# One transfer for a unit's rows, and a first weight matrix laid out as 128 long rows

## The chip, the cores and the metric

The kernel runs on one core of one Trainium2 chip. The metric is device time in microseconds (us) of one execution, taken as the median of several runs. Five engines work side by side on a core: TensorE (PE, with its weight loads shown apart as PEld), VectorE (DVE), ScalarE (ACT), GpSimd (POOL) and SyncE (SP), which here only issues transfers. The core has 16 DMA engines that move the bytes.

## The reference

Three layers follow each other. The first is a gated linear attention over 4 batches x 8 heads x 768 tokens of 40 values; its output is the 3,072 x 320 matrix that the second layer takes.

```python
for t in range(S):
    m_new = np.maximum(f_gate[:, :, t] + m, i_gate[:, :, t])
    f_stab = np.exp(f_gate[:, :, t] + m - m_new)
    i_stab = np.exp(i_gate[:, :, t] - m_new)
    C = f_stab * C + i_stab * outer(vt, kt);  n = f_stab * n + i_stab * kt
    y[:, :, t] = sigmoid(o_gate[:, :, t]) * (C @ qt) / np.maximum(np.abs(n @ qt), 1.0)
...
logits = x @ w_gate            # 8 experts, each takes its 384 best tokens, greedily
out[mask] = np.maximum(x[mask] @ w1[e], 0.0) @ w2[e]
...
h = x @ w_in                   # 320 x 2048, the "first weight matrix" (win)
g = np.where(h > 0.0, h, np.exp(np.minimum(h, 0.0)) - 1.0)
return g @ w_out               # 2048 x 320 (wout)
```

The weights `w_in` and `w_out` arrive as 8-byte floats and are turned into 4-byte ones on the chip.

## The kernel before

**Attention** runs over 24 units. A unit `u` is one chunk of 64 tokens (`n = u // 2`) of one pair of batches (`bp = u % 2`); the 128 partitions of its output tile `x` hold the 64 tokens of the one batch and the 64 of the other, the two in swapped order, since `values` and `recall` write to the opposite half (`64 - r`). `Attention.run` (L480 to L549) writes the order of all engines' work out by hand. In each unit it loads `vk` for unit u+4 and `qk` for unit u+5, both on SP's queue, multiplies, divides by the denominators in `gates` (L423, the last step is on POOL at L434), stores the unit's 128 rows of 320 values to the DRAM tile `xd` in `rows_out` (L436), and pulls one more piece of the late layers' weights (`pull`). The tile `x` has three buffers, `vk` six, `qk` four, a weight piece `cx` three.

**Weight pieces.** `win_pieces` (L987) brings in 15 pieces during attention: pieces 0 to 9 are `win`, pieces 10 to 14 the first part of `wout`. Each is loaded as 8-byte words (`fetch`, L942), turned into 4-byte floats (`conv`, L948) and split in two. Pieces 0 to 7 are 128 rows of 512 words. Pieces 8 and 9 are the last 64 rows of `win`, folded so that they fill 128 partitions: each has one transfer for the lower 64 partitions and one for the upper.

**SP's queue** runs in order. Each transfer on it uses one of eight semaphores in turn and waits until the transfer eight places ahead of it has landed.

**After attention** the router picks each expert's tokens (`Router.round`); the first round ends with gathers of rows from `xd` (`get_x`). Then the two expert layers run, eight rounds of 384 tokens each. The remaining nine pieces of `wout` (tile `wx`) are loaded from the end of attention on, behind the last store on SP's queue.

Of the kernel before, what the change touches and what calls it, by code (L numbers as in the profile page):

```python
# [16 lines left out]
B, H, S, D = 4, 8, 768, 40  # L17
# [102 lines left out]
class Attention:  # L120
# [315 lines left out]
    def rows_out(self, u):  # L436

        nc = self.nc
        n, bp = divmod(u, 2)
        x = self.st["x", u]  # L440
        for r in range(2):
            row = (bp * 2 + 1 - r) * S + n * 64
            nc.sync.dma_start(self.xd[row:row + 64], x[r * 64:r * 64 + 64])

    def turn(self, u):
        x = self.st.pop(("x", u))
# [105 lines left out]
class Router:  # L552
# [9 lines left out]
    def tables(self):  # L562
        nc, c, stage = self.nc, self.c, self.stage
        G, V = nc.gpsimd, nc.vector
        kw = dict(allow_small_or_imprecise_dtypes=True)
        self.pc = c.tile([128, 1], F32, name="pc")
        for r in (0, 64):
            G.iota(self.pc[r:r + 64], pattern=[[0, 1]], base=0, channel_multiplier=1, **kw)
        self.mul3 = c.tile([128, 3], F32, name="mul3")
        G.memset(self.mul3, -256.0)  # L570
        G.memset(self.mul3[:, 2:], -64.0)
        self.add3 = c.tile([128, 3], F32, name="add3")
        G.iota(self.add3[:, :2], pattern=[[128, 2]], base=2048, channel_multiplier=1, **kw)
        for h in (0, 64):
            G.iota(self.add3[h:h + 64, 2:], pattern=[[0, 1]], base=512, channel_multiplier=1, **kw)
        self.kx = c.tile([128, 32, 6], BF, name="kx")
        G.iota(self.kx, pattern=[[1, 32], [0, 6]], base=0, channel_multiplier=0, **kw)
        self.kl = c.tile([128, 16, 2], BF, name="kl")
        G.iota(self.kl, pattern=[[2, 16], [1, 2]], base=0, channel_multiplier=0, **kw)
        self.w8 = c.tile([128, 8], F32, name="w8")  # L580
        G.iota(self.w8, pattern=[[1, 8]], base=1, channel_multiplier=0, **kw)
        self.colv = c.tile([128, 24], BF, name="colv")
        for r in (0, 64):
            G.iota(self.colv[r:r + 64].rearrange("p (a b c) -> p a b c", a=2, b=2), pattern=[[64, 2], [2 * S, 2], [128, 6]],
                   base=(1 - r // 64) * S, channel_multiplier=0, **kw)
        jt = stage.tile([128, 128], I32, name="jt", bufs=1)
        G.iota(jt, pattern=[[1, 128]], base=0, channel_multiplier=0)
        d = stage.tile([128, 128], F32, name="tri0", bufs=1)
        G.iota(d, pattern=[[1, 128]], base=0, channel_multiplier=-1, **kw)
        self.ones = c.tile([128, 128], BF, name="ones")  # L590
        G.memset(self.ones, 1.0)
        self.onz = c.tile([128, 128], BF, name="onz")
        G.memset(self.onz, 64.0)
        G.memset(self.onz[0:1], 0.0)
        self.one48 = c.tile([128, 48], F32, name="one48")
        G.memset(self.one48, 1.0)
        self.ax = c.tile([128, 24], F32, name="ax")
        self.flag = [c.tile([128, 8], BF, name=f"flag{i}") for i in range(2)]
        for x in self.flag:
            G.memset(x, 0.0)  # L600
        yield
        self.thr0 = stage.tile([128, 128], I32, name="thr0", bufs=1)
        m = stage.tile([128, 128], I32, name="tblt", bufs=1)
        V.tensor_scalar(jt, jt, 25, None, op0=ALU.logical_shift_left)
        yield
        V.tensor_scalar(m, jt, 31, -1, op0=ALU.arith_shift_right, op1=ALU.bitwise_xor)
        yield
        V.tensor_scalar(m, m, -2**31, None, op0=ALU.bitwise_or)
        yield
        V.tensor_tensor(self.thr0, jt, m, op=ALU.bitwise_xor)  # L610
        yield
        V.memset(self.thr0[:, 0:1].bitcast(F32), -3.4e38)
        self.tri = c.tile([128, 128], BF, name="tri")
        V.tensor_scalar(self.tri, d, 0.0, -1.0, op0=ALU.is_gt, op1=ALU.add)
        yield
        self.far = c.tile([128, 128], BF, name="far")
        V.tensor_scalar(self.far, d, 0.0, -4096.0, op0=ALU.is_equal, op1=ALU.mult)
# [291 lines left out]
class Mlp:  # L909
# [77 lines left out]
    def win_pieces(self, stage):  # L987

        nc = self.nc
        A, G = nc.scalar, nc.gpsimd  # L990
        wide = self.win.dtype != F32
        n = 512
        al, lo, up = slice(0, 128), slice(0, 64), slice(64, 128)
        tiles = {}
        total = 10 + EARLY * 320 // 448
        self.piece = self.got = 0

        def whole():
            return stage.tile([128, n], F32, name="cF")

        def get(i):
            k, h = divmod(i, 4)
            cs = slice(h * n, h * n + n)
            tiles[i] = [stage.tile([128, n, 2], I32, name="cx", bufs=3) if wide else None, None, None if wide else whole()]
            if i >= 10:
                cs = slice((i - 10) * 448, (i - 10) * 448 + 448)
                tiles[i] = [t if t is None else t[:, :448] for t in tiles[i]]
                loads = [(al, self.src(self.wout, al, cs))]
            elif k < 2:
                loads = [(al, self.src(self.win, slice(k * 128, k * 128 + 128), cs))]  # L1010
            else:
                w = self.src(self.win, slice(256, 320), slice(h * 1024, h * 1024 + 1024))
                w = w.rearrange("p (k e t) -> e p k t", k=4, e=2)
                loads = [(lo, w[0]), (up, w[1])]
            self.fetch(loads, wide, tiles[i])

        def pull():
            if self.got < min(total, self.piece + 2 + wide):
                get(self.got)
                self.got += 1  # L1020

        self.pull = pull
        for i in range(total):
            self.piece = i
            while i not in tiles:
                yield
            k, h = divmod(i, 4)
            cs = slice((i - 10) * 448, (i - 10) * 448 + 448) if i >= 10 else slice(h * n, h * n + n)
            if wide:
                w = 448 if i >= 10 else n  # L1030
                tiles[i][1:] = stage.tile([128, n], F32, name="cg")[:, :w], whole()[:, :w]
            F = tiles[i][2]
            yield from self.conv(wide, tiles.pop(i), top=True)
            if i >= 10:
                A.activation(self.first[0][:, cs], F, AF.Copy)
                yield
                nc.vector.tensor_tensor(self.first[1][:, cs], F, self.first[0][:, cs], op=ALU.subtract)
            elif k < 2:
                A.activation(self.wih[:, k, cs], F, AF.Copy)
                yield  # L1040
                G.tensor_tensor(self.wil[:, k, cs], F, self.wih[:, k, cs], op=ALU.subtract)
            else:
                w = self.wis.rearrange("p (k e t) -> p k e t", e=2, t=128)[:, 4 * h:4 * h + 4]
                F = F.rearrange("p (k t) -> p k t", t=128)
                A.activation(w[lo, :, 0], F[lo], AF.Copy)
                yield
                A.activation(w[up, :, 1], F[up], AF.Copy)
                yield
                nc.vector.tensor_tensor(w[up, :, 0], F[lo], w[lo, :, 0], op=ALU.subtract)
                yield  # L1050
                nc.vector.tensor_tensor(w[lo, :, 1], F[up], w[up, :, 1], op=ALU.subtract)
            yield
# [500 lines left out]
def kernel(ctx, tc, qk, vk, ig, fg, wg, w1a, w1b, w2a, win, wout, out):  # L1553
# [22 lines left out]
    rt.__init__(nc, tc, consts, wk, L, sp, plan)  # L1576
    tables = rt.tables()
    next(tables)

    def hook(u):  # L1580
# [32 lines left out]
def _layout(i):  # L1613

    import numpy as np

    def by_dim(a):
        return a.reshape(2, 2, 8, 12, 64, 40).transpose(3, 1, 5, 0, 2, 4)

    def by_token(a):  # L1620
        return a.reshape(2, 2, 8, 12, 64, 40).transpose(3, 1, 4, 0, 2, 5)

    def words(a):
        a = np.ascontiguousarray(a)
        return a.view(np.uint64) if a.dtype == np.float64 else a

    d = {}
# [4 lines left out]
    v = by_token(i["v"])  # L1632
    v = np.concatenate([v, np.ones((*v.shape[:-1], 1), v.dtype)], -1)
# [6 lines left out]
    d["w1a"] = i["moe_w1"][:, :256].reshape(2048, 1024)  # L1640
    d["w1b"] = i["moe_w1"][:, 256:].reshape(512, 1024)
    d["w2a"] = i["moe_w2"].reshape(8, 2, 4, 128, 320).transpose(0, 1, 3, 2, 4).reshape(2048, 1280)
    d["win"] = words(i["moe2_w_in"])
    d["wout"] = words(i["moe2_w_out"].reshape(16, 128, 320).transpose(1, 0, 2).reshape(128, 5120))
    return {n: np.ascontiguousarray(a) for n, a in d.items()}

# [16 lines left out]
```

## Time and profile before

| | |
|---|---|
| median of 3 runs | 755.16 us (752.74 to 759.88) |
| profiled execution | 750.71 us |
| its span, first to last instruction | 748.9 us |
| PE busy | 702.9 us (94%) |
| DVE / ACT / POOL busy | 541.3 / 377.6 / 186.6 us |
| mean granted TensorE clock | 0.969 of full speed |

The table is read from the first part of the profile: the share of the span in which each engine is busy. PE is busy nearly throughout, but a mean over the span hides that the stages differ: attention takes the first 150 us, the router's first round some 35, the expert layers the rest.

### The profile page before, as it was taken

The numbers are of one execution on the slowest core, as the hardware profiler recorded it, in microseconds if no ns is written. First come the engines' busy times: TensorE is split into PE (matmuls) and PEld (weight loads), VectorE is DVE, ScalarE is ACT, GpSimd is POOL, SyncE is SP. The second block draws the span as 40 slices with busy tenths as digits, with TensorE's granted clock in tenths as the row PEclk, the third lists the DMA queues.
The fourth block names the chain that finished last, engine by engine and source line by source line (L and its number), as shares of the span: only waits on it lengthen the run. The fifth ranks groups of instructions, "written<-read, shape, count | busy, mean of one in ns | idle before, by whom it ended". The sixth has DMA issues, their size and how long they took to land.

```text
span 748.9 us, 17930 instructions
## 1 busy us (share of the span) xinstructions
PE 702.9 (94%) x7274; PEld 639.3 (85%) x7274; DVE 541.3 (72%) x1592; ACT 377.6 (50%) x804; POOL 186.6 (25%) x242
## 2 busy tenths in 40 slices
PE   7889888837999999999999999999999999999997
PEld 4656666626989999999999999999999999999997
DVE  8687888887898968965896698569868833851442
ACT  5455445435365725842772366256527743752443
POOL 5666655235111401210301120112022220001001
PEclk9899999957999999999999999999999999999999
DMA  7777968236002301400320230022013321100000
GB/s 280 237 231 226 251 212 261 51 109 214 18 1 85 124 1 51 131 28 1 103 80 28 85 93 5 27 85 98 1 30 109 112 88 45 36 1 26 1 2 27
DMA packets 22436, 67.31 MB, mean 90 GB/s; under 512 B 3536, under 2 KB 7632, under 8 KB 22352
## 3 DMA queue, kind: packets, MB, share of 16 engines
q1 hardware_dynamic: 14240, 35.12, 15.4%
q0 software_dynamic: 8064, 30.94, 12.4%
q8 instruction: 57, 0.93, 0.5%
q14 instruction: 27, 0.22, 0.1%
q10 hardware_dynamic: 48, 0.10, 0.0%
HBM read 58.28 MB, written 7.86 MB: 88 GB/s over the span
## 4 chain that ended last, share of the span: by engine, by line
PE 73%; issue 11%; DVE 9%; ACT 3%; POOL 2%; DMA 1%; POOLq 0%; SPq 0%; ACTq 0%; DVEq 0%
PE ph L1223 30%; PE acc L1362 6%; PE acc L1366 6%; PE acc L1363 6%; PE acc L1330 3%; PE acc L1332 3%; PE acc L1331 2%; PE pO L381 2%; PE pR L395 2%; PE pX L464 2%; PE acc L1317 1%; PE acc L1319 1%; PE pX L450 1%; PE pr L807 1%; PE pO L365 1%
## 5 line engine op out<-in xcount | busy, mean ns | idle before, releaser
L1276 DVE SCALAR_TENSOR_TENSOR e<-e,ph 128x384 f32<-128x384 f32 x128 | 70.3, 550 | 50.4 <-ACT e L1273 49.7
L1272 ACT ACTIVATE e<-ph 128x384 f32<-128x384 f32 x128 | 62.5, 488 | 79.4 <-PE ph L1223 74.3
L1223 PE MATMUL ph<-yh,wih 128*128 128x384 f32 x256 | 89.1, 348 | 0.7 <-DVE xl L1184 0.4
L1240 ACT ACTIVATE gh<-ph 128x384 fp32r<-128x384 f32 x64 | 31.3, 491 | 114.0 <-PE ph L1223 89.1
L1223 PE MATMUL ph<-yh,wil 128*128 128x384 f32 x256 | 86.1, 337 | 0.0
L1375 POOL DMA_INDIRECT out_dram<-ot,idx x24 | 24.0, 998 | 210.8 <-ACT ot L1093 207.8
L1100 DVE TENSOR_TENSOR gl<-e,gh 128x384 fp32r<-128x384 f32 x128 | 70.9, 561 | 1.8 <-ACT gh L1093 0.3
L1273 ACT ACTIVATE e<-e 128x384 f32<-128x384 f32 x128 | 67.3, 526 | 4.0
L1362 PE MATMUL acc<-woh,gh 128*128 128x320 f32 x216 | 68.3, 316 | 0.0
L1247 DVE SCALAR_TENSOR_TENSOR gl<-ph,gh 128x384 fp32r<-128x384 f32 x64 | 35.2, 552 | 45.5 <-ACT gh L1240 45.3
L1366 PE MATMUL acc<-woh,gl 128*128 128x320 f32 x216 | 66.9, 310 | 0.5 <-DVE gl L1100 0.5
L1363 PE MATMUL acc<-wol,gh 128*128 128x320 f32 x216 | 66.8, 309 | 0.0
L1223 PE MATMUL ph<-yl,wih 128*128 128x384 f32 x256 | 66.0, 338 | 0.0
L1093 ACT ACTIVATE gh<-e 128x384 fp32r<-128x384 f32 x96 | 49.0, 514 | 11.4 <-DVE e L1276 11.1
L1366 PE MATMUL acc<-woa,gl 128*128 128x320 f32 x168 | 52.4, 312 | 0.9 <-DVE gl L1100 0.9
L1362 PE MATMUL acc<-woa,gh 128*128 128x320 f32 x168 | 52.8, 314 | 0.0
L1223 PEld LDWEIGHTS ph<-yh,wih 128*128 128x128 f32 x256 | 48.1, 188 | 4.8 <-ACT yh L1335 4.1
L1363 PE MATMUL acc<-wob,gh 128*128 128x320 f32 x168 | 51.8, 308 | 0.0
L1223 PEld LDWEIGHTS ph<-yh,wil 128*128 128x128 f32 x256 | 48.1, 188 | 0.0
L1104 POOL DMA_INDIRECT stg<-in_w1a_dram,wi x16 | 15.7, 983 | 123.3 <-DVE wi L845 119.0
L1223 PEld LDWEIGHTS ph<-yl,wih 128*128 128x128 f32 x256 | 46.1, 188 | 0.0
L1223 PE MATMUL ph<-xh,w1h 128*128 128x384 f32 x128 | 44.6, 349 | 0.1
(290 smaller groups left out, 2041.4 us busy)
## 6 DMA issues: line engine op xcount, KB each, us to landing
vk<-in_vk_dram SPq DMA_DIRECT2D x24, 484.0 KB, 5.4
qk<-in_qk_dram SPq DMA_DIRECT2D x20, 320.0 KB, 5.5
cx<-in_win_dram SPq DMA_DIRECT2D x8, 512.0 KB, 5.1
xd<-x SPq DMA_DIRECT2D x48, 80.0 KB, 3.4
wx<-in_wout_dram SPq DMA_DIRECT2D x9, 320.0 KB, 3.0
cx<-in_wout_dram SPq DMA_DIRECT2D x5, 448.0 KB, 4.1
qk<-in_qk_dram SPq DMA_DIRECT2D x4, 512.0 KB, 6.1
cx<-in_win_dram SPq DMA_DIRECT2D x4, 256.0 KB, 5.7
```

The source lines that it names most:

```text
L1093: self.nc.scalar.activation(out, x, AF.Copy)
L1100: self.nc.vector.tensor_tensor(out, x, y, op=ALU.subtract)
L1223: PE.matmul(p, w, x, start=k == 0, stop=k == 7)
L1240: nc.scalar.activation(h, p, AF.Relu)
L1247: nc.vector.scalar_tensor_tensor(l, p, 0.0, h, op0=ALU.max, op1=ALU.subtract)
L1272: nc.scalar.activation(e, p, AF.Relu, scale=-1.0)
L1273: nc.scalar.activation(e, e, AF.Exp, scale=-1.0)
L1276: nc.vector.scalar_tensor_tensor(e, e, -1.0, p, op0=ALU.add, op1=ALU.max)
L1362: PE.matmul(p, h[:, c], wh, start=f == 0, stop=False)
L1363: PE.matmul(p, h[:, c], wl, start=False, stop=False)
L1366: PE.matmul(p, l[:, c], wh, start=False, stop=f == 15)
L1375: s = nc.gpsimd.indirect_dma_start(out=self.out, out_offset=bass.IndirectOffsetOnAxis(ap=idx[:, t:t + 1], axis=0), in_=o, in_offset=None)
```

## The change

`rows_out` stores a unit's rows in one transfer. For this the two batches of a pair change places in the inputs (q, k, v and the gates), so that after the swap inside the kernel partition half `r` belongs to batch `r`; on the DRAM side the 128 rows are then two blocks of 64 rows, 768 rows apart. The router's table of token numbers (`colv`) follows. `win` is laid out as 128 rows of 5,120 words: the first 128 rows of the matrix, the second 128, and the last 64 folded, side by side; so pieces 8 and 9 are loaded like the others, in one transfer of 128 rows each.

```diff
@@ -438,9 +438,8 @@  rows_out
         n, bp = divmod(u, 2)
         x = self.st["x", u]
-        for r in range(2):
-            row = (bp * 2 + 1 - r) * S + n * 64
-            nc.sync.dma_start(self.xd[row:row + 64], x[r * 64:r * 64 + 64])
+        rows = self.xd[bp * 2 * S:bp * 2 * S + 2 * S].rearrange("(r s) d -> r s d", r=2)
+        nc.sync.dma_start(rows[:, n * 64:n * 64 + 64], x)
@@ -582,7 +581,7 @@  Router.tables
             G.iota(self.colv[r:r + 64].rearrange("p (a b c) -> p a b c", a=2, b=2), pattern=[[64, 2], [2 * S, 2], [128, 6]],
-                   base=(1 - r // 64) * S, channel_multiplier=0, **kw)
+                   base=r // 64 * S, channel_multiplier=0, **kw)
@@ -999,19 +998,14 @@  win_pieces, get
-            k, h = divmod(i, 4)
-            cs = slice(h * n, h * n + n)
+            cs = slice(i * n, i * n + n)
             tiles[i] = [stage.tile([128, n, 2], I32, name="cx", bufs=3) if wide else None, None, None if wide else whole()]
             if i >= 10:
                 cs = slice((i - 10) * 448, (i - 10) * 448 + 448)
                 tiles[i] = [t if t is None else t[:, :448] for t in tiles[i]]
                 loads = [(al, self.src(self.wout, al, cs))]
-            elif k < 2:
-                loads = [(al, self.src(self.win, slice(k * 128, k * 128 + 128), cs))]
             else:
-                w = self.src(self.win, slice(256, 320), slice(h * 1024, h * 1024 + 1024))
-                w = w.rearrange("p (k e t) -> e p k t", k=4, e=2)
-                loads = [(lo, w[0]), (up, w[1])]
+                loads = [(al, self.src(self.win, al, cs))]
             self.fetch(loads, wide, tiles[i])
@@ -1614,6 +1608,10 @@  _layout
+    i = dict(i)
+    for n in ("q", "k", "v", "i_gate", "f_gate", "o_gate"):
+        i[n] = i[n].reshape(2, 2, *i[n].shape[1:])[:, ::-1].reshape(i[n].shape)
@@ -1640,7 +1638,8 @@
-    d["win"] = words(i["moe2_w_in"])
+    w = i["moe2_w_in"]
+    d["win"] = words(np.concatenate([w[:128], w[128:256], w[256:].reshape(64, 8, 2, 128).transpose(2, 0, 1, 3).reshape(128, 1024)], 1))
```

On PE, DVE, ACT and POOL the same instructions stand in the same order as before. Only SP's queue differs: it has 99 rows in place of 125. The two fences below show it at two places, by the order of the built program; a row names the tile written, the one read, the shape of the DRAM side, outermost count first, and in brackets what the transfer waits for (`DMAHW0` to `DMAHW7` are the eight semaphores of the queue's transfers, `Pool`, `DVE` and `Activation` those of the engines).

SP's queue in the middle of attention before, from the store of unit 9 to that of unit 10:

```order
L443 DMA xd<-x 64x320 [waits DMAHW2_49,Pool_49]
L443 DMA xd<-x 64x320 [waits DMAHW3_49]
L946 DMA cx<-in_win_dram 64x4x256 [waits DMAHW4_49,Activation_49]
L946 DMA cx<-in_win_dram 64x4x256 [waits DMAHW5_49]
L282 DMA vk<-in_vk_dram 128x968 [waits DMAHW6_49,DVE_49]
L278 DMA qk_114<-in_qk_dram 80x1024 [waits DMAHW7_49,DVE_49]
L443 DMA xd<-x 64x320 [waits DMAHW0_49,Pool_49]
L443 DMA xd<-x 64x320 [waits DMAHW1_49]
```

The same place with the change:

```order
L442 DMA xd<-x 2x64x320 [waits DMAHW1_49,Pool_49]
L945 DMA cx<-in_win_dram 128x1024 [waits DMAHW2_49,Activation_49]
L282 DMA vk<-in_vk_dram 128x968 [waits DMAHW3_49,DVE_49]
L278 DMA qk_114<-in_qk_dram 80x1024 [waits DMAHW4_49,DVE_49]
L442 DMA xd<-x 2x64x320 [waits DMAHW5_49,Pool_49]
```

Two stores of 64 rows have become one whose outermost count is 2, and the two loads of piece 8 one of 128 rows. Since a unit now has four transfers, the eighth transfer ahead is the same kind of transfer two units earlier.

SP's queue at the end of attention with the change, from the last load for attention (`vk` of unit 23) to the first loads of the rest of `wout`:

```order
L282 DMA vk<-in_vk_dram 128x968 [waits DMAHW4_49,DVE_49]
L442 DMA xd<-x 2x64x320 [waits DMAHW5_49,Pool_49]
L442 DMA xd<-x 2x64x320 [waits DMAHW6_49,Pool_49]
L442 DMA xd<-x 2x64x320 [waits DMAHW7_49,Pool_49]
L442 DMA xd<-x 2x64x320 [waits DMAHW0_49,Pool_49]
L442 DMA xd<-x 2x64x320 [waits DMAHW1_49,Pool_49]
L945 DMA wx<-in_wout_dram 128x640 [waits DMAHW2_49,Activation_49]
L945 DMA wx<-in_wout_dram 128x640 [waits DMAHW3_49,DVE_49]
L945 DMA wx<-in_wout_dram 128x640 [waits DMAHW4_49]
```

The five stores of units 19 to 23 stand there where ten transfers of 64 rows stood, and the `wx` loads still follow right behind.

## Rows read from the trace of the kernel before

**Rows 1.** The page's 40 equal slices of the span, in tenths.

```profile
PE   7889888837999999999999999999999999999997
DMA  7777968236002301400320230022013321100000
```

**Rows 2.** Busy time by stage (us); the last three columns are granted clock, DMA share, GB/s.

```profile
0.00:20.00 20.00, 14.83 (x281) 8.89 (x285) 16.78 (x39) 10.56 (x24) 10.81 (x43) 1.00 0.80 280
20.00:150.00 130.00, 113.03 (x3189) 84.22 (x3189) 103.78 (x247) 65.19 (x134) 69.55 (x71) 0.93 0.71 209
150.00:185.00 35.00, 18.73 (x163) 14.58 (x164) 26.46 (x93) 13.63 (x31) 16.72 (x17) 0.62 0.51 161
185.00:749.00 564.00, 556.36 (x3650) 531.66 (x3648) 394.25 (x1215) 288.17 (x616) 89.48 (x112) 1.00 0.16 51
136.50:148.00 11.50, 9.85 (x204) 8.24 (x202) 10.16 (x30) 4.22 (x12) 2.19 (x3) 1.00 0.20 46
```

**Rows 3.** The page's chain that ended last, by engine and by line.

```profile
PE 73%; issue 11%; DVE 9%; ACT 3%; POOL 2%; DMA 1%; POOLq 0%; SPq 0%; ACTq 0%; DVEq 0%
PE ph L1223 30%; PE acc L1362 6%; PE acc L1366 6%; PE acc L1363 6%; PE acc L1330 3%; PE acc L1332 3%; PE acc L1331 2%; PE pO L381 2%; PE pR L395 2%; PE pX L464 2%; PE acc L1317 1%; PE acc L1319 1%; PE pX L450 1%; PE pr L807 1%; PE pO L365 1%
```

**Rows 4.** Timeline of SP's queue: start, us, what was issued.

```profile
19.17 1.15 SPq L443 DMA_DIRECT2D xd<-x  x2
...
31.13 1.09 SPq L443 DMA_DIRECT2D xd<-x  x2
...
39.28 1.09 SPq L443 DMA_DIRECT2D xd<-x  x2
...
128.16 0.33 SPq L282 DMA_DIRECT2D vk<-in_vk_dram  x1
130.76 17.99 SPq L443 DMA_DIRECT2D xd<-x  x10
148.84 1.49 SPq L946 DMA_DIRECT2D wx<-in_wout_dram  x3
```

**Rows 5.** DMA view: SP's queue q1, and its transfers (count, KB each, us to landing).

```profile
q1 hardware_dynamic: 14240, 35.12, 15.4%
...
vk<-in_vk_dram SPq DMA_DIRECT2D x24, 484.0 KB, 5.4
qk<-in_qk_dram SPq DMA_DIRECT2D x20, 320.0 KB, 5.5
cx<-in_win_dram SPq DMA_DIRECT2D x8, 512.0 KB, 5.1
xd<-x SPq DMA_DIRECT2D x48, 80.0 KB, 3.4
...
cx<-in_wout_dram SPq DMA_DIRECT2D x5, 448.0 KB, 4.1
...
cx<-in_win_dram SPq DMA_DIRECT2D x4, 256.0 KB, 5.7
```

**Rows 6.** The tile xd: its stores and its gathers (min/median/max ns, first and last start).

```profile
L443 SPq DMA_DIRECT2D xd<-x x48: 445/508/1762, 19.2 to 148.2; - x48
L1104 POOL DMA_INDIRECT xg<-xd,idx x24: 942/950/1405, 174.1 to 598.4; - x24
...
DMA to landing us min/median/max: 2.0/3.1/6.2
```

**Rows 7.** Timeline of ACT: the last unit's gates from its vk tile, first use of wx.

```profile
141.50 0.47 ACT L355 ACTIVATE sg<-vk 128x320 f32<-128x320 f32 x1
...
152.15 0.48 ACT L958 ACTIVATE wt<-wx 128x320 f32<-128x320 f32 x1 [1.58 <-DMA wx<-in_wout_dram]
```

**Rows 8.** Busy time in two neighbouring stretches of attention, columns as in Rows 2.

```profile
24.00:31.00 7.00, 4.13 (x108) 2.93 (x111) 5.40 (x12) 5.99 (x12) 3.76 (x3) 0.93 0.80 245
31.00:39.00 8.00, 8.00 (x212) 6.12 (x212) 3.57 (x10) 2.31 (x5) 3.65 (x5) 0.63 0.64 178
```

**Rows 9.** The list of waits: POOL's step in gates behind stores.

```profile
POOL x L434 <- DMA xd<-x: 7.3, 3, 2.9
```

## The prediction

> **What bounds the kernel now.** I read the 40 slices first [rows 1]. PE is near nine tenths everywhere but in a hole around slices 9 and 10; the DMA line is high in slices 1 to 7 and low after them. So the transfers matter in attention, if anywhere. The table by stage says how much [rows 2]: from 185 us on PE is busy 556.36 of 564 us, and the chain that ended last is mostly the experts' matmuls [rows 3]. Nothing that the change touches works in that stage, so it moves as a block. From 20 to 150 us PE is busy 113.03 of 130 us, DVE 103.78, and the 16 DMA engines 0.71 of the time. Attention is thus close to three limits at once. Its pace is read from SP's queue [rows 4]: the store of unit 0 is issued at 19.17 us, that of unit 19 at 130.76, which is 111.59 / 19 = 5.87 us a unit. What delays the end of attention delays everything behind it.
>
> **Part by part: pieces 8 and 9.** Four loads of 256 KB become two of 512 KB. Same bytes; a 512 KB piece lands in 5.1 us, a 256 KB half in 5.7 [rows 5]. Rows of 40 KB pitch, as `win` now has, are what `wout` has already, and its 448 KB pieces land in 4.1 us, so the pitch costs nothing. The pieces are read long after they land. I count 0; two SP issues of some 0.5 us are saved on a queue that mostly waits for POOL and DVE.
>
> **The inputs' swap and the iota's base** change values, not instructions: 0.
>
> **The store.** Before, a unit has two stores of 80 KB, 64 rows each; all 48 are issued in 445 to 1762 ns and land 2.0 us after issue at best, 3.1 in the median [rows 6]. Now one of 160 KB. What decides is over how many of the 16 engines it is dealt out. Every transfer on SP's queue before has an outermost count that 16 divides (128, 80, 64, 32 rows), and none shows an engine left out. The new store is the first whose DRAM side has an outermost count of 2: two blocks of 64 rows. If a transfer is dealt out by whole outermost entries, two engines carry 64 rows each and 14 carry none.
>
> The Trainium skill says this outright (DMA: Bandwidth & Descriptors, section "Why a DMA increments its semaphore by 16 and not by 1"): the number of engines is the largest one up to 16 that divides the slowest dimension of both sides. By it the store runs on two engines. No run here shows such a transfer yet.
>
> I take two engines as likeliest, and price it. Bytes per engine and unit: `vk` 484/16 = 30.3 KB, `qk` 320/16 = 20.0, pieces (10 x 512 + 5 x 448)/16 over some 20 units = 23.0; together 73.3 KB. The stores add 10 KB to each of 16 engines before, and 80 KB to each of two after.
>
> What an engine moves while busy has three rows. In the first 20 us, loads alone, 280 GB/s at share 0.80 is 280/(16 x 0.80) = 21.9 GB/s, or 21.4 KB/us [rows 2]. Over all of q1, 35.12 MB in 15.4% of 16 x 748.9 us is 19.0 GB/s, 18.6 KB/us [rows 5]. From 136.5 to 148 us, where nearly all traffic is stores, 46/(16 x 0.20) = 14.4 GB/s, 14.0 KB/us [rows 2]. As a check, 83.3 KB at 18.6 is 4.5 us of a 5.87 us unit, 0.76; the table has 0.71.
>
> On the two engines a unit then takes:
> - low: everything at 21.4, 73.3/21.4 + 80/21.4 = 3.4 + 3.7 = 7.2 us;
> - middle: loads at 21.4, since the other 14 engines are idle half the time, and stores at 18.6, 64 packets in a row being nearer to the mean of the queue than to its short bursts: 3.4 + 4.3 = 7.7 us;
> - high: loads at 18.6, stores at 14.0, 3.9 + 5.7 = 9.6 us.
>
> Each load spreads over all 16 engines, so it lands only when the two slow ones have done their part; the unit's pace becomes theirs. Over the present 5.87 us that is +1.3, +1.86, +3.8 us a unit, and over 19 units with loads +25, +35, +72 us.
>
> Against this stands the lead of the loads. The last `vk` is issued at 128.16 us and lands 5.4 us later [rows 4, 5]; ACT reads it at 141.50 [rows 7]. So 141.5 - 133.6 = 7.9 us can pass before anything waits. Left: +17, +27, +64 us. SP's own waits put no further brake on: a transfer waits for the one eight ahead, which is now two units back, and two units of transfers in flight keep both engines fed.
>
> **The end of attention.** Units 20 to 23 have no loads; they take 17 us from 130.76 to the store's last issue at 148.2 [rows 4, 6]. Four stores on two engines take 4 x 3.7 to 4 x 5.7 = 15 to 23 us, in the middle 17: no change there. But the first `wx` load is issued right behind the last store and ACT waited 1.58 us for it already [rows 7], so no slack is left: the last store's 4.3 us in place of 80 KB over 16 engines (10/18.6 = 0.5) delays it by some 3 us (0 to 6). That wait passes to the router's round through ACT and DVE. The gathers of `xd` begin at 174.1 us, 26 us after the last store's issue [rows 6], more than its landing takes.
>
> **The clock.** After a stretch with PE busy 4.13 of 7.00 us the granted clock was 0.63 over the next 8 us, part of them at 1.2 GHz in place of 2.4, and the unit there took 39.28 - 31.13 = 8.15 us with PE busy throughout [rows 4, 8]. At 7.7 us a unit PE would be busy 5.1 of them (113.03/130 x 5.87), 66%, near that 59%. So some units will run at 8.15 in place of 7.7: at most 19 x 0.4 = 8 us, I take 4; nothing at the high end, where 9.6 us covers it.
>
> **Sum.** Low 17 + 0 + 0 = +17; middle 27 + 3 + 4 = +34; high 64 + 6 + 0 = +70 us. Against the profiled execution, 750.7 + 34 = 785 us; the median of the runs lies 4.4 us above that execution, so 755.2 + 34 = 789 us for a median.
>
> **Rivals.**
>
> *All 16 engines carry the store* (the 128 partitions of `x` decide, not the two blocks). Then 10 KB per engine and unit as before, and one SP issue of some 0.5 us less each unit. For it speaks that both forms move the same 128 rows of 1,280 bytes. It gives 755 us, not slower. The most it could win: POOL's step in `gates` is put down as waiting 7.3 us for stores, in three places [rows 9]; if all of it were theirs and went, 748 us, 1.0% faster. But POOL's operand comes from DVE's step just ahead of it (L433), and a wait for several is put down to the one that came last, so I believe little of it.
>
> The Trainium skill's "Rules for kernel authors" on the same page advise this side: small transfers are to be joined, and two halves of the partitions to be made one transfer. Taken alone that would give the 755 us here or a little less.
>
> *Two engines, but hidden.* The lead covers 7.9 us in 19 units, 0.4 us a unit. So a unit could take 6.3 us on the two engines and nothing would be seen: with loads at 3.4 that leaves 2.9 us for 80 KB, 28 KB/us, faster than any row's 21.4. It decides below that rate, and gives 755 to 760 us.
>
> *Deeper trouble.* Landing times on the two engines grow to two units, 15 us, about the distance between a piece's load and its first use; if ACT, in order, then stands at a piece's conversion, the unit waits for more than its bytes. That is past the high end: 825 us and up.
>
> **How the numbers follow.** Two engines and visible: 0.72, since the built program carries the count of 2 and every row before agrees with a deal by whole outermost entries without proving it. All 16 engines: 0.20. Two engines but hidden: 0.05. Deeper trouble: 0.03. The likeliest case alone spans 755 + 17 to 755 + 70, 772 to 825; packets could move a little faster than the slow rows say when 14 engines stand idle, so its own weight lies in the lower half. To hold 8 in 10 the range must reach into the case of 16 engines: from 754, which leaves out about half of that case, 0.10, to 816, which leaves out 0.08. About 1% is what a measurement of this kernel can tell from no change, its runs lying 752.74 to 759.88 us apart. Faster by over 1% is only the top of the first rival, 0.03; within 1% the rest of it and the hidden case, 0.22; slower 0.75.
>
> **What would show it.** Right: the `xd` stores land in 7 us or more in place of 3.1; `vk`, `qk` and pieces land in 10 us or more; the mean DMA share from 20 to 150 us falls well under 0.71; SP's queue waits for transfers; units are 7 to 8 us apart; the experts' stage keeps its 556 us of PE. Wrong: stores landing in about 3 us, and units still 5.9 us apart. If the stores land late but units keep their pace, the lead was larger than I read; if units pass 9.6 us, a wait behind an in-order engine adds to the bytes.

## The result, and the profile after

| | before | with the change |
|---|---|---|
| median | 756.82 us (4 runs) | 762.28 us (4 runs, 760.43 to 767.01) |
| ratio | | 1.0106, 95% interval 1.0063 to 1.0149 |
| profiled execution | 750.71 us | 760.43 us |
| its span | 748.9 us | 758.6 us |

The change makes the kernel slower by about 1%, 8 us by the ratio. The forecast was 789 us, 34 more than before, with a range of 754 to 816: the sign and the mechanism hold, the size does not. The unaltered kernel, run again in the experiments (run 7), gave 1.0095. The profiled execution of before, 750.71 us, lies under all four of its runs here, so the two spans differ by more, 9.7 us, than the medians do.

The page's slices of the changed kernel answer to [rows 1]:

```profile
PE   7898888754999999999999999999999999999997
DMA  7776666225300500500230121022003321100000
```

The high part of the DMA line is as long as before, but one to three tenths lower in three of its seven slices, and the hole in PE begins a slice earlier and is wider: 7, 5, 4 in slices 8 to 10, before 8, 3, 7. The table by stage answers to [rows 2] and [rows 8]; its last three columns are the granted clock, the DMA share and GB/s:

```profile
0.00:20.00 20.00, 15.44 (x276) 9.65 (x276) 16.36 (x38) 10.34 (x24) 10.11 (x42) 0.91 0.79 269
20.00:150.00 130.00, 110.62 (x3120) 81.36 (x3118) 99.24 (x223) 63.50 (x129) 66.82 (x70) 0.92 0.63 207
185.00:749.00 564.00, 560.27 (x3655) 533.65 (x3655) 400.00 (x1224) 291.91 (x624) 92.73 (x113) 1.00 0.16 54
...
142.00:150.00 8.00, 5.62 (x91) 4.43 (x85) 5.05 (x12) 3.83 (x10) 1.03 (x1) 0.79 0.13 45
...
149.00:156.70 7.70, 6.09 (x86) 5.22 (x86) 5.46 (x20) 1.92 (x6) 1.46 (x2) 0.88 0.13 42
```

From 144 to 157 us, when the last load has landed, only stores are left. In the last two rows the 16 engines have a mean share of 0.13, which is 2 of 16, and move 45 and 42 GB/s. I read this as two engines at some 22 GB/s each and 14 idle ones. Before, the same stores moved 46 GB/s at a share of 0.20 [rows 2], so the share alone does not count engines; the packets do, in runs 3 and 4. The queue's packets and its store row answer to [rows 5]:

```profile
q1 hardware_dynamic: 12720, 35.12, 14.1%
...
xd<-x SPq DMA_DIRECT2D x24, 160.0 KB
```

Of the 14,240 packets 1,520 are gone for the same 35.12 MB: 768 because pieces 8 and 9 come in packets of 4 KB in place of 1 KB, the other 752 smaller than 512 bytes. Times to landing are read here from the chain, the waits and the times at which the trace has each transfer's completions. SP's queue, to be held against [rows 4]:

```profile
19.89 0.63 SPq L442 DMA_DIRECT2D xd<-x  x1
...
49.76 0.50 SPq L442 DMA_DIRECT2D xd<-x  x1
...
129.93 0.49 SPq L442 DMA_DIRECT2D xd<-x  x1
130.51 2.83 SPq L945 DMA_DIRECT2D cx<-in_wout_dram  x1
133.43 2.14 SPq L282 DMA_DIRECT2D vk<-in_vk_dram  x1
135.67 20.98 SPq L442 DMA_DIRECT2D xd<-x  x5
156.74 1.36 SPq L945 DMA_DIRECT2D wx<-in_wout_dram  x3
```

The five stores from 135.67 on are those of units 19 to 23. From the store of unit 0 to that of unit 19 it is 115.78 us, before 111.59: +4.2. From there to the first `wx` load it is 21.07 us, before 18.08: +3.0. The store of unit 0 itself is 0.7 later. The first gather of `xd` comes at 183.8 us in place of 174.1 [rows 6], another +1.8 behind the `wx` load:

```profile
L442 SPq DMA_DIRECT2D xd<-x x24: 482/497/1737, 19.9 to 156.2; - x24
L1098 POOL DMA_INDIRECT xg<-xd,idx x24: 948/954/1414, 183.8 to 608.1; - x24
```

From that gather to the last instruction both kernels take 574.8 us. So the 9.7 us between the two spans are 0.7 + 4.2 + 3.0 + 1.8, all of them ahead of the experts' layers. These are single executions. Before and the kernels below with no store on two engines (runs 2, 3, 4, 6 and 11) took 111.0 to 119.0 us from the store of unit 0 to that of unit 19, so the 4.2 is not clear of their spread. From there to the first `wx` load they took 16.3 to 18.3 us, so the 3.0 is clear of it; from that load to the gather they took 25.3 to 26.8 against 27.1 here, so the 1.8 hardly is.

The list of waits, from the store of unit 0 to the router (us in total, times, longest):

```profile
ACT cg L957 <- DMA cx<-in_wout_dram: 8.2, 2, 5.0
PEld pS L306 <- DMA qk<-in_qk_dram: 7.7, 7, 1.8
...
ACT wt L957 <- DMA wx<-in_wout_dram: 2.8, 1, 2.8
```

Engines now wait for loads, ACT for weight pieces and PE for `qk`. The chain that ended last shows the longest of these waits, in unit 20 (start, us, what):

```profile
130.51 12.59 DMA cx<-in_wout_dram
143.12 0.05 ACT cg L957
```

The last weight piece is issued at 130.51 us, behind the store of unit 18 on the two engines, and lands 12.6 us later; before, such a piece took 4.1 us in the median [rows 5]. Of its 16 completions 14 are there by 136.44 us, the other two come at 140.43 and 143.10: two engines hold it back. ACT, in order, has nothing else to do:

```profile
143.12 0.60 ACT L957 ACTIVATE cg<-cx 128x448 f32<-128x448 f32 x1 [5.03 <-DMA cx<-in_wout_dram]
```

### The profile page after: what moved, and what is told of

Same layout as the page of the kernel before. It is cut to its first block, busy times and chain, and to the rows that moved or that the text cites. A ratio compares the mean times of both kernels' runs of the same rounds, so it can differ in the third digit from the quotient of the medians.

```text
span 758.6 us, 17883 instructions
## 1 busy us (share of the span) xinstructions
PE 709.1 (93%) x7274; PEld 644.2 (85%) x7274; DVE 542.7 (72%) x1592; ACT 377.8 (50%) x804; POOL 184.8 (24%) x242
## 2 busy tenths in 40 slices
DMA packets 20915, 67.30 MB, mean 89 GB/s; under 512 B 2784, under 2 KB 5856, under 8 KB 20832
## 3 DMA queue, kind: packets, MB, share of 16 engines
q1 hardware_dynamic: 12720, 35.12, 14.1%
## 4 chain that ended last, share of the span: by engine, by line
PE 70%; DVE 10%; issue 10%; DMA 6%; ACT 2%; POOL 1%; POOLq 0%; SPq 0%; ACTq 0%; DVEq 0%
PE ph L1217 30%; PE acc L1356 6%; PE acc L1360 6%; PE acc L1357 6%; PE acc L1324 3%; DMA qk<-in_qk_dram 3%; PE acc L1326 2%; PE acc L1325 2%; PE pR L395 2%; PE pO L381 2%; DMA cx<-in_wout_dram 2%; PE pX L463 2%; PE acc L1311 1%; PE acc L1313 1%; PE pS L306 1%
## 5 line engine op out<-in xcount | busy, mean ns | idle before, releaser
L1087 ACT ACTIVATE gh<-e 128x384 fp32r<-128x384 f32 x96 | 49.0, 514 | 11.5 <-DVE e L1270 11.1
L1098 POOL DMA_INDIRECT stg<-in_w1a_dram,wi x16 | 15.8, 986 | 123.3 <-DVE wi L844 119.0
```

The lines of the kernel that those rows point to most:

```text
L1087: self.nc.scalar.activation(out, x, AF.Copy)
```

## The experiments

All ratios are to the kernel before, run on the same chip beside them. Lines that begin with "-" are those of the changed kernel.

**1. The changed store alone.** `win`'s layout and its loads are those of before.

```diff
-                loads = [(al, self.src(self.win, al, cs))]
+            elif k < 2: loads = [(al, self.src(self.win, slice(k * 128, k * 128 + 128), cs))]
+            else: ... loads = [(lo, w[0]), (up, w[1])]
-    d["win"] = words(np.concatenate([w[:128], w[128:256], ...], 1))
+    d["win"] = words(i["moe2_w_in"])
```

> The changed store alone, with the first weight matrix laid out and loaded as before. Theory (the store runs on two of the 16 engines, and their time decides): all of the loss is here, the ratio to before is 1.006 to 1.015 as with the whole change, and during the last units the DMA share is 0.13, two of 16. Rival (the new layout of the weight matrix or its 512 KB pieces cost the time): the time is that of before, ratio 0.995 to 1.005.

Measured: 768.72 us, ratio 1.0184 (1.0157 to 1.0211). The loss is all in the store, and it is larger without the new layout than with it, which neither theory said.

**2. The new layout alone.** The rows go out in two transfers as before.

```diff
-        rows = self.xd[bp * 2 * S:bp * 2 * S + 2 * S].rearrange("(r s) d -> r s d", r=2)
-        nc.sync.dma_start(rows[:, n * 64:n * 64 + 64], x)
+        for r in range(2):
+            row = (bp * 2 + r) * S + n * 64
+            nc.sync.dma_start(self.xd[row:row + 64], x[r * 64:r * 64 + 64])
```

> The new layout of the first weight matrix alone; a unit's rows go out in two transfers of 64 rows as before. Theory (two engines): ratio to before 0.995 to 1.005, units of 5.9 us, and no stretch in which the DMA share stands at 0.13. Rival (layout): ratio 1.006 to 1.015.

Measured: 752.95 us, ratio 0.9978 (0.9949 to 1.0006): no difference that can be told.

**3 and 4. The same single transfer over four and over 16 engines.** Only the number of blocks on the DRAM side changes.

```diff
-        rows = self.xd[bp * 2 * S:bp * 2 * S + 2 * S].rearrange("(r s) d -> r s d", r=2)
-        nc.sync.dma_start(rows[:, n * 64:n * 64 + 64], x)
+        rows = self.xd.rearrange("(r s) d -> r s d", r=4)      # run 4: r=16, and 8 rows in place of 32
+        nc.sync.dma_start(rows[:, u * 32:u * 32 + 32], x)
```

> The whole change, but the rows' side in DRAM is four blocks of 32 rows in place of two of 64, still one transfer a unit; rows stand at other places in the matrix between the layers, so the output's rows are exchanged, the work is the same. Theory: four engines carry 32 rows each, some 1.8 us a unit beside some 2.9 us of loads, 4.7 us in all, under the unit's own 5.9; so the time of before, ratio 0.993 to 1.006, and a DMA share of 0.25 where stores run alone. Rival (one transfer of 160 KB, or its blocks with gaps, cost the time, not the number of engines): still 1.006 to 1.015.

> As with four blocks, but 16 blocks of 8 rows, one transfer a unit (the output's rows are exchanged likewise). Theory: all 16 engines carry 8 rows each, as before the change; ratio to before 0.990 to 1.005, and the same time as with the four blocks to within 0.5%, since with four the store was already under the unit's own time. Rival (one transfer costs the time): 1.006 to 1.015.

Measured: 749.86 us, 0.9928 (0.9903 to 0.9952) with four blocks; 751.89 us, 0.9967 (0.9943 to 0.9991) with 16. The loss is gone in both, though each is one transfer of 160 KB in blocks with gaps. That rival falls; the count of blocks is what matters. Four engines are no slower than 16, as expected once the store fits under the unit. Here and in runs 5 and 6 the rows stand at places that the router's table does not name, so the output is not the reference's; the work is the same.

How many engines carry a store shows in the count of the smallest packets. The page's lines for the changed kernel, for four blocks and for 16 blocks:

```profile
DMA packets 20915, 67.30 MB, mean 89 GB/s; under 512 B 2784, under 2 KB 5856, under 8 KB 20832
DMA packets 20963, 67.30 MB, mean 90 GB/s; under 512 B 2832, under 2 KB 5904, under 8 KB 20880
DMA packets 21251, 67.30 MB, mean 90 GB/s; under 512 B 3120, under 2 KB 6192, under 8 KB 21168
```

Only the 24 stores differ, and the packets under 512 bytes are 2,784, 2,832 and 3,120: 2 more a store with four blocks and 14 more with 16. Run 5, with 24 stores of two blocks more, has 2,832, 48 more than the changed kernel, so such a store has 2. That fits one such packet for each of 2, 4 and 16 engines. One expectation failed: the DMA share where stores run alone was not 0.25 with four blocks but 0.15 from 130 to 147 us: a store's packets take some 2.3 us there of the 4 between two stores, and the engines then idle.

The Trainium skill's rule on the number of engines (DMA: Bandwidth & Descriptors, "Why a DMA increments its semaphore by 16 and not by 1") agrees with these runs: slowest dimensions of 2, 4 and 16 gave 2, 4 and 16 such packets a store. The advice of the same page of the Trainium skill to make one transfer out of two halves ("Rules for kernel authors") did no harm here with four and with 16 blocks; with two it cost 1%.

**5 and 6. The store doubled,** on two engines and on 16.

```diff
-        rows = self.xd[bp * 2 * S:bp * 2 * S + 2 * S].rearrange("(r s) d -> r s d", r=2)
-        nc.sync.dma_start(rows[:, n * 64:n * 64 + 64], x)
+        for xd in (self.xd, self.twin):
+            rows = xd.rearrange("(r s) d -> r s d", r=2)      # run 6: r=16, and 8 rows in place of 64
+            nc.sync.dma_start(rows[:, u * 64:u * 64 + 64], x)
```

> The dose doubled on two engines: each unit's rows are stored once more, into a second matrix that nothing reads, both transfers as two blocks of 64 rows (blocks 1,536 rows apart, so the output's rows are exchanged). Theory, sized by the trace of the changed kernel (two engines at 22.5 GB/s each, 3.6 us a store): the two engines then have 7.2 us of stores and some 2.9 us of loads in a unit, 10.1 against the 5.9 that a unit takes on its own; over 19 units 80 us less the lead of some 8, and 10 to 18 us more at the end, ratio to before 1.09 to 1.13. Rival (a 160 KB transfer has a price of its own, not bound to two engines): the loss of the change once more, ratio 1.02 to 1.03.

> The same double store, but each as 16 blocks of 8 rows (the output's rows are exchanged, the second copy is not read). Theory: 10 KB more for each of 16 engines, some 0.5 us a unit on engines that were busy about three quarters of the time: ratio 0.99 to 1.01. Rival (one more transfer or its bytes cost, on whatever engines): 1.02 or more.

Measured: 834.45 us, ratio 1.102 (1.0982 to 1.1058) on two engines; 755.56 us, 0.9977 (0.9951 to 1.0003) on 16. This is the run that gives the price. SP's queue with the double store on two engines:

```profile
54.29 0.50 SPq L443 DMA_DIRECT2D xd<-x  x1
...
196.22 0.49 SPq L443 DMA_DIRECT2D xd<-x  x1
...
214.70 3.18 SPq L443 DMA_DIRECT2D xd<-x  x1
217.93 3.22 SPq L443 DMA_DIRECT2D twin<-x  x1
221.25 3.17 SPq L443 DMA_DIRECT2D xd<-x  x1
224.47 3.22 SPq L443 DMA_DIRECT2D twin<-x  x1
227.78 4.37 SPq L946 DMA_DIRECT2D wx<-in_wout_dram  x3
```

At the end only stores are in flight, and each transfer waits for the eighth ahead of it to land. So they pass at the pace of the two engines: 214.70 to 227.78 is four stores, 3.27 us each, 80 KB an engine, 24.5 KB/us. From unit 4 to unit 19 a unit takes (196.22 - 54.29)/15 = 9.46 us. Two stores are 6.54 of that; 2.92 us are left for loads. SP's queue issues 11 pieces, 15 `vk` and 14 `qk` there, 71 KB an engine and unit, so 24.3 KB/us. The stretch with stores alone, and the waits:

```profile
200.00:210.00 10.00, 5.47 (x51) 4.26 (x51) 5.15 (x12) 3.40 (x8) 0.89 (x1) 0.65 0.13 51
```

```profile
PEld pS L306 <- DMA qk<-in_qk_dram: 39.8, 12, 5.0
...
ACT cg L958 <- DMA cx<-in_win_dram: 37.2, 8, 9.5
...
ACT wt L958 <- DMA wx<-in_wout_dram: 14.2, 1, 14.2
```

Again 0.13, two engines, now 51 GB/s; and the same three waits as in the changed kernel, several times as long.

**7. The changed kernel again,** unaltered.

> The changed kernel unaltered, to compare it with the changed store alone on equal terms, since that came out at 1.0184 where the whole change had 1.0106. If the new layout of the weight matrix wins back time beside the narrow store, this is again 1.006 to 1.015; if the two differ by chance alone, 1.014 to 1.021.

Measured: 763.46 us, ratio 1.0095 (1.0064 to 1.0127). So the gap to the changed store alone, 1.0157 to 1.0211, is real: beside the narrow store, the new layout wins back some 0.9%.

**8. A longer lead for the weight pieces.**

```diff
-            tiles[i] = [stage.tile([128, n, 2], I32, name="cx", bufs=3) if wide ...
+            tiles[i] = [stage.tile([128, n, 2], I32, name="cx", bufs=4) if wide ...
-            if self.got < min(total, self.piece + 2 + wide):
+            if self.got < min(total, self.piece + 3 + wide):
-        self.VK[u] = self.two.tile([128, 968], F32, name="vk", bufs=6)
+        self.VK[u] = self.two.tile([128, 968], F32, name="vk", bufs=5)
```

> The changed kernel with a fourth buffer for weight pieces, each asked for one unit earlier (and five buffers for vk in place of six, for room). Theory: the last piece's late landing, behind which ACT stood for 5.0 us in the changed kernel, is covered, and ACT's waits for pieces fall from 8.2 us to under 2; the pace of the units stays near 6.1 to 6.2 us, since the two engines set it; so 2 to 5 us less than the changed kernel. Rival (no landing matters by itself, only the bytes on the two engines): the same time as the changed kernel to within 2 us, the wait moving to other loads.

Measured: 759.51 us, ratio 1.003 (1.0008 to 1.0051), 3.9 us under the changed kernel run beside it. ACT's waits for pieces are gone from the list; of its waits for loads in attention this is left, with PE's for `qk`:

```profile
ACT wt L957 <- DMA wx<-in_wout_dram: 4.6, 1, 4.6
PEld pS L306 <- DMA qk<-in_qk_dram: 1.6, 4, 0.8
```

The units from 5 to 18 keep their pace, 49.83 to 130.90 us, 6.24 each. What was won lies behind them:

```profile
136.21 17.50 SPq L442 DMA_DIRECT2D xd<-x  x5
153.81 1.57 SPq L945 DMA_DIRECT2D wx<-in_wout_dram  x3
```

From the store of unit 19 to the first `wx` load it is 17.6 us; the changed kernel took 21.07, before 18.08. So the 3.0 us after unit 19 were ACT standing at the last piece and what came of it; the fall of the granted clock to 0.79 behind the stand, from 142 to 150 us, is not parted from the stand itself. The theory holds. The buffers of `vk` were changed too, which this run does not part from the pieces' lead.

**9 and 10. What the new layout wins back.** Pieces 8 and 9 in two transfers with packets of 4 KB, or in one with packets of 1 KB.

```diff
-                loads = [(al, self.src(self.win, al, cs))]
+                loads = [(p, self.src(self.win, p, cs)) for p in ((al,) if i < 8 else (lo, up))]      # run 9
+                if i >= 8: w = self.src(self.win, al, slice(4096, 5120)).rearrange("p (k j t) -> j p k t", k=4, j=2)[i - 8]      # run 10; ... win is laid out to match
```

> The changed kernel, but pieces 8 and 9 of the first weight matrix come in two transfers of 64 rows each, still in packets of 4 KB. It splits what the changed store alone lost more than the whole change (1.0184 against 1.0095). Theory (the number of packets on the two slow engines counts): as the changed kernel, 1.006 to 1.013. Rival (the number of transfers counts, since each waits for the eighth ahead of it): near the changed store alone, 1.014 to 1.021.

> The changed kernel, but pieces 8 and 9 come in packets of 1 KB (four to a row), still in one transfer of 128 rows each. Theory (packets on the two slow engines count): 32 packets of 1 KB on each engine in place of 8 of 4 KB for each of the two pieces, the ratio rises to 1.014 to 1.021. Rival (the number of transfers counts): as the changed kernel, 1.006 to 1.013.

Measured: 767.72 us, 1.0131 (1.0092 to 1.017), with two transfers; 765.92 us, 1.0112 (1.0072 to 1.0151), with 1 KB packets. Both intervals touch that of the changed kernel, and the first that of the changed store alone. So neither edit is the whole of it, and the split stays open. One execution of each points to two parts. The first lies ahead of unit 19: from the store of unit 0 to that of unit 19 run 1 takes 121.5 us and run 9 120.0, both with pieces 8 and 9 in two transfers; run 10, in one, takes 116.0, the changed kernel 115.8 and again 116.8. The second is one thing that runs 9, 10 and 1 share, and that the changed kernel lacks, in units 21 to 23. In run 1 they look like this, to be held against the row from 149.00 to 156.70 of the changed kernel above:

```profile
154.00:165.40 11.40, 10.12 (x89) 8.76 (x89) 5.48 (x20) 1.73 (x5) 1.47 (x2) 0.50 0.11 35
```

The granted clock is 0.50, the lower level of 1.2 GHz, over the whole stretch, and 89 weight loads and matmuls keep PE busy 10.12 us; in the changed kernel's row 86 take 6.09. It takes 11.4 us in place of 7.7. In runs 9 and 10 the stretch takes 11.5 and 11.2 us at 0.50, in the changed kernel run again 7.7 at 0.89. In all of them ACT had stood in unit 20 for the last piece; in these three the clock then stayed down until attention was over. That is 3.7 of the 6 to 7 us between run 1 and the changed kernel. Why the clock recovered in one and not in the others was not tried.

**11. One transfer over 16 engines with the reference's output.** The matrix between the layers holds each unit's 128 rows side by side, and the scatter's token numbers are worked out from the places.

```diff
-        rows = self.xd[bp * 2 * S:bp * 2 * S + 2 * S].rearrange("(r s) d -> r s d", r=2)
-        nc.sync.dma_start(rows[:, n * 64:n * 64 + 64], x)
+        nc.sync.dma_start(self.xd[u * 128:u * 128 + 128], x)
-  ... pattern=[[64, 2], [2 * S, 2], [128, 6]], base=r // 64 * S
+  ... pattern=[[256, 2], [128, 2], [512, 6]], base=r
+        ...
+        V.tensor_scalar(nq[:, 0], idx, 6, 3, op0=ALU.logical_shift_right, op1=ALU.bitwise_and)
+        V.tensor_scalar(nq[:, 1], idx, 8, None, op0=ALU.logical_shift_right)
+        V.scalar_tensor_tensor(odx, nq[:, 0], 704.0, idx, op0=ALU.mult, op1=ALU.add)
+        V.scalar_tensor_tensor(odx, nq[:, 1], -192.0, odx, op0=ALU.mult, op1=ALU.add)
+        ...
```

> One transfer a unit over all 16 engines with the reference's output: the matrix between the layers holds each unit's 128 rows side by side, the gathers use these places, and four small operations on VectorE a round turn a place back into the token's number for the scatter. Theory: no narrow store, so the time of before or a little less, as with 16 blocks: ratio 0.992 to 1.002, the four operations costing under 1 us in the first round and hidden in the others. Rival (the four operations stand on the router's path in every round): 1.003 or more.

Measured: 751.28 us, ratio 0.992 (0.9888 to 0.9953). It is faster than both kernels, and like run 3. The store's row in its tile xd:

```profile
L441 SPq DMA_DIRECT2D xd<-x x24: 319/326/798, 20.3 to 149.2; - x24
```

Where the 0.8% come from was not followed further: its profiled execution, of span 750.8 us, is no shorter than the one of before, 748.9.

## Why the sign was right and the size wrong

**Two engines: right, and shown.** The count of small packets, the last of a load's 16 completions 3 to 7 us behind the 14th (before at most 1.2), the loss that vanishes with four or 16 blocks, and the loss that grows from 1% to 10% when the narrow store is doubled, while the same double store on 16 engines costs nothing. Of the signs that the prediction named, the late landings came: from unit 5 to unit 18 the stores land 9.7 to 12.5 us after issue, loads 8.2 to 13.4. The DMA share fell only to 0.63, SP's queue waited for no transfer in attention, and units took 6.2 us, not 7 to 8.

**What an engine moves: the step that failed.** The forecast priced the two engines from rows in which all 16 worked together, 21.4, 18.6 and 14.0 KB/us, and took 7.7 us a unit. Two engines kept full moved 24.5 KB/us of stores and 24.3 of loads (run 5): 3.27 + 2.92 = 6.19 us a unit. The changed kernel's units from 5 to 18 took (129.93 - 49.76)/13 = 6.17 us. The pace alone would prove little, since run 6, with no store on two engines, took 6.26 in its one profile. But in the changed kernel's trace the last completions of all transfers from unit 5 to unit 18 follow each other with next to no gap: a store's comes 3.2 us behind the one ahead of it, a `vk`'s mostly 1.2, a `qk`'s 0.7 to 1.1, a piece's 1.1 to 1.3. So the slower of the two engines was kept full, at run 5's price, and the term of +35 us was mis-sized: at 6.19 it is (6.19 - 5.87) x 19 = 6 us. In all the narrow store costs some 1.3%, 10 us, when the changed kernel (1.0095) is held against the one with 16 blocks (0.9967). For the doubled store 9.46 us a unit gives (9.46 - 5.87) x 19 = 68 us. Less the 7.9 of lead, and with 14.2 us of waiting for `wx` in place of 1.58, the forecast's sum comes to 73 us there; 834.45 - 756.36 = 78 were measured.

**The lead: too generous.** At 6 us the 7.9 us of lead should have covered everything. It was read from `vk`, whose last load has the most room. PE waited for `qk` and ACT for weight pieces instead. How much of the 4.2 us up to unit 19 is theirs the single executions do not tell.

**The clock in attention: not seen where it was put.** From 20 to 150 us it is 0.92, before 0.93. It matters behind the stand in unit 20: 0.79 from 142 to 150 us, and 0.50 through the last three units of runs 1, 9 and 10.

**The end of attention: right in kind.** The first `wx` load is waited for 2.8 us in place of 1.58 [rows 7], and 1.8 us in all, hardly more than the spread of single executions, are lost between it and the gathers; 3 were forecast. Not forecast were the 3.0 us ahead of it, which go with ACT's stand at the last piece (run 8).

**Pieces 8 and 9: right alone, wrong together.** Alone the new layout changes nothing (run 2). Beside the narrow store it wins back some 0.9%; the forecast counted 0.

**The rivals.** All 16 engines: no. Hidden: by its own bound of 6.3 us a unit this was nearly the case that came, and it was given 0.05, because its 28 KB/us was derived with loads held at the forecast's slower price. Deeper trouble named the wait that did occur, ACT at a piece's conversion, but as something beyond the high end; it came at the low one.

## What to carry to other kernels

Before joining two transfers, read the joined one's outermost count on both sides: here two blocks put the whole transfer on two of 16 engines, and every later load waits for those two. Price engines that are kept full from a stretch in which they are kept full, and not from a mean over all 16. A mean DMA share does not count engines: four showed as 0.15 here. A lead is that of the load with the least room, and an engine that works in order loses the whole of one late landing at once.

## What was not expected of the hardware

- Two engines kept full moved 24.3 to 24.5 KB/us each (run 5); over the whole queue before, with all 16 at work, the mean was 18.6.
- A load on all 16 engines landed with its last two: in the changed kernel 14 of a piece's 16 completions took 5.9 us from issue, the last 12.6.
- SP issues the plain 128-row store in 326 ns in the median, the one of two blocks in 497 ns (`xd` views of run 11 and of the changed kernel), one half of 64 rows before in 508 ns [rows 6].
- After the stand in unit 20 the granted clock was 0.50 through the last three units in three kernels and 0.88 to 0.89 in the changed kernel's two profiles, 11.2 to 11.5 us against 7.7 for the same units.
